# The first tile's load split over two DMA queues, and shorter idle matmuls ahead of it

## The chip, the core and the metric

The kernel runs on one NeuronCore of a Trainium2 chip. TensorE multiplies matrices from SBUF into PSUM, VectorE and ScalarE work on tiles, GpSimd does the rest, and SyncE issues most DMAs. ScalarE has a DMA queue of its own as well. The metric is the device time of one execution in microseconds (us); the median of three runs of the kernel before is 210.25 us (210.12 to 210.37).

## The reference

The input x has 2048 rows of 512 bf16 values. It is normalised row by row, and the result goes through linear attention of 32 heads and through a gated feed-forward layer of width 1792. Both are added to x.

```python
def _layernorm(x, axis=-1, eps=1e-5):
    m = jnp.mean(x, axis=axis, keepdims=True)
    v = jnp.var(x, axis=axis, keepdims=True)
    return (x - m) / jnp.sqrt(v + eps)

# linear attention: phi on q and k, k'v and the sum of k first, then q against them
phi = lambda t: jnp.where(t > 0, t + 1, jnp.exp(t)) + 1e-6
# feed-forward
(silu(x @ w_gate) * (x @ w_up)) @ w_down

xn = _layernorm(A_x)
return A_x + _A_ref(xn, A_wqkv, A_wo) + _B_ref(xn, B_w_gate, B_w_up, B_w_down)
```

## The kernel before

The 2048 rows are 16 tiles of 128 rows, one row to a partition. The program is written out by hand as one list of operations for each engine. A small planner (`_Prog`) keeps, for each named resource such as ("x", 0), who wrote it last and who has read it since; from that it derives every semaphore wait. Each engine works its own list strictly in order, so the place of a line in the source sets the order only among operations of the same engine. Each DMA has its own semaphore.

In the long run TensorE does, for each tile, the projections to k and q (line 438, with `kproj` and `qproj`), accumulates k'v (line 590), and later works the feed-forward layer (line 785) and the output (lines 979 and 990). The start is different, because nothing is in SBUF yet. The steps that matter are these.

- **Loads** (lines 199 to 262). SyncE loads tile 0 of x as its first DMA (line 250), then chunks 0 and 1 of the key weights in one load of 256 KB, chunk 2, tile 2, and so on. ScalarE's queue has two loads, tile 1 (line 239) and chunk 3 of the key weights (line 252). Ahead of them ScalarE has one Exp on a single column, which brings in its table (line 236). The load of tile 1 is declared as a reader of `ident`, so it waits for the memset of that tile on GpSimd (line 238), and GpSimd's next write of `ident`, the select that makes the identity matrix (line 242), waits until that load has landed.
- **Idle matmuls** (`fill`, line 267). TensorE begins with eight matmuls of constants, 512 columns wide, whose result nobody reads (line 610), and has one of 128 columns among the transposes (line 620).
- **Tile 0**: VectorE takes the statistics (`bns`, line 299, and `agg`, line 302) and subtracts the mean in two halves of the columns into `xc_sb` (`xc_half`, line 382). TensorE transposes each half against `ident` in two matmuls (`tp_first`, line 410), ScalarE copies it into `xcT` (`tc_first`, line 422).
- **Tile 1**: ScalarE takes the mean itself (`mean_act`, line 307), VectorE subtracts it after tile 0's halves, and the same transposes and copies follow.
- **First projections** (`proj_part`, line 465): one matmul for each chunk of the weights, for tile 0 in the order of chunks 0, 1, 3, 2, then the same for tile 1, then parts of the query projections. Tile 2 comes in after twelve of them, with four transposes.

The factor of the variance is put in later, by ScalarE's reading of the projections (`first_ek` and the like), so the transposes needn't wait for it. GpSimd computes it (`eps` and `rstd_of`) after `ident` and a memset of two values.

Of the kernel before, what the change touches and what calls it, by code (L numbers as in the profile page):

```python
# [10 lines left out]
P = 128  # L11
# [98 lines left out]
def bass_parallel_sum__linear_attn_block__swiglu_ffn__prompt_kernel(  # L110
# [10 lines left out]
    xin = A_x[0]  # L121
    oview = out[0]
    K = _Prog()
    pe, act, dve, pool, sp = nc.tensor, nc.scalar, nc.vector, nc.gpsimd, nc.sync
    bf, f32 = dt.bfloat16, dt.float32

    with contextlib.ExitStack() as es:
        E = es.enter_context

        def sb(name, shape, d=bf):  # L130
            return E(nc.sbuf_tensor(name, [P] + shape, d))

        x_sb = sb("x_sb", [NT, D])
# [14 lines left out]
        stats = sb("stats", [NT, 6], f32)  # L148
# [43 lines left out]
        def bk(i):  # L192
            return ("bank", i)
# [5 lines left out]
        def rows(v, t0, n):  # L199
            if t0 < NLONE:  # L200
                return v[t0 * P:(t0 + n) * P, :].rearrange("(t p) d -> p t d", p=P)
            return v[NLONE * P:, :].rearrange("(p t) d -> p t d", t=NT - NLONE)[:, t0 - NLONE:t0 - NLONE + n, :]

        def xload(eng, h, t0, n, after=()):
            K.dma(
                eng, lambda: h.dma_start(x_sb[:, t0:t0 + n, :], rows(xin, t0, n)),
                r=list(after), w=[("x", t0 + i) for i in range(n)],
            )

        def wqkv_load(eng, h, name, i, c0, n, after=()):  # L210
            K.dma(
                eng,
                lambda: h.dma_start(
                    wqkv_sb[:, c0:c0 + n, i * D:(i + 1) * D],
                    A_wqkv[c0 * P:(c0 + n) * P, i * D:(i + 1) * D].rearrange("(c p) f -> p c f", p=P),
                ),
                r=list(after), w=[(name, c) for c in range(c0, c0 + n)],
            )
# [6 lines left out]
        def whalf(name, dst, src, h):  # L225
# [6 lines left out]
                w=[(name, h)],  # L232
            )

        K.op("pool", lambda: pool.memset(warm[:, :], 0.0), w=[("warm",)])
        K.op("act", lambda: act.activation(warm[:, :], warm[:, :], ACT.Exp), r=[("warm",)], w=[("warm",)])

# [8 lines left out]
            r=[("ident",)], w=[("ident",)],  # L246
        )
        K.op("pool", lambda: pool.memset(nhalf[:, :], -0.5), w=[("nhalf",)])

        xload("sp", sp, 0, 1)  # L250
        wqkv_load("sp", sp, "wk", 1, 0, 2)
        wqkv_load("act", act, "wk", 1, 3, 1)
        wqkv_load("sp", sp, "wk", 1, 2, 1)
# [13 lines left out]
        def fill(n, cols, after=()):  # L267
            K.op(
                "pe",
                [  # L270
                    (lambda: pe.matmul(banks[3][:, 0:cols], cw, cx[:, 0:cols], start=True, stop=True))  # L271
                    for _ in range(n)
                ],
                r=list(after), w=[bk(3)],
            )
# [20 lines left out]


        def bns(t):
            K.op("dve", lambda: dve.bn_stats(stats[:, t, :], x_sb[:, t, :]), r=[("x", t)], w=[("st", t)])  # L299

        def agg(t):
            K.op("dve", lambda: dve.bn_aggr(mv[:, t, :], stats[:, t, :]), r=[("st", t)], w=[("mv", t)])
# [296 lines left out]
        def stat(t):  # L599
            bns(t)  # L600
            agg(t)
            eps(t, "pool")
            rstd_of(t)
# [3 lines left out]
            if t >= 3:  # L607
                transpose_dma(t)

        fill(8, 512)  # L610
        bns(0)
        agg(0)
        xc_half(0, 0)
# [10 lines left out]
        tp_first(1, 0, 6)  # L624
        tc_first(1, 0, 6)
        bns(1)
        rstd_of(0)
        xn_dve(0)
# [459 lines left out]
```

## Time and profile before

| | |
|---|---|
| median of 3 runs | 210.25 us (210.12 to 210.37) |
| the profiled execution | 210.51 us, of which 209.3 us are the span that the profile covers |
| TensorE busy | 206.6 us, 99% of the span |
| VectorE / ScalarE / GpSimd busy | 57% / 34% / 34% |
| DMA | 16.84 MB, mean 80 GB/s |

All times in a profile line are us from the start of the span, unless marked ns. In the timeline a line holds the start, the length, the engine, the source line and the operation with its tiles; neighbours of the same kind are merged (x3), the length is then from the first one's start to the last one's end, and the square bracket tells how long the engine had been idle before and what ended that. A question about a short window shows pieces that a longer one merges. PE is TensorE, PEld its loading of weights, DVE VectorE, ACT ScalarE, POOL GpSimd; SPq and ACTq are the issues of DMAs on SyncE's and ScalarE's queues. Matmuls are pipelined: the next one can start before the one before has its end in the profile.

### The profile page before, as it was taken

The page shows a single profiled execution, that of the slowest core. Times are in us where ns is not written, and L with a number is a line of the kernel's source. Part 1 is how long each engine was busy: PE and PEld are TensorE (multiplying, and loading weights), DVE is VectorE, ACT ScalarE, POOL GpSimd, SP SyncE. Part 2 cuts the span into 40 slices and gives each one's busy share as a digit, 9 for nine tenths or more (in the row PEclk, how much of TensorE's full clock was granted, in tenths as well). Part 3 has the DMA queues.
Part 4 walks back from the last instruction along what each step waited for, and adds up shares of the span by engine and source line. Part 5 has one row for each costly group of instructions (what it writes and reads, how often), then busy time and mean ns, then how long its engine had stood idle before and what let it go on. Part 6 is the DMA issues. An engine that isn't in the chain of part 4 may idle for free.

```text
span 209.3 us, 2824 instructions
## 1 busy us (share of the span) xinstructions
PE 206.6 (99%) x1015; PEld 94.6 (45%) x1015; DVE 120.2 (57%) x246; ACT 70.9 (34%) x125; POOL 72.0 (34%) x90
## 2 busy tenths in 40 slices
PE   8999999999999999999999999999999999999996
PEld 3444444444444444444444444444444444444444
DVE  3999988336365874637355746365556545374122
ACT  5777666966643331312112312213031213121000
POOL 3427977568032543223041422240424132221200
PEclk9999999999999999999999999999999999999999
DMA  6673644894797011010101110102011010110101
GB/s 200 209 195 75 127 100 100 256 364 158 202 357 50 11 39 25 28 25 25 50 2 50 28 29 22 50 0 53 6 45 25 27 28 25 49 30 25 50 28 50
DMA packets 30287, 16.84 MB, mean 80 GB/s; under 512 B 20928, under 2 KB 29632, under 8 KB 30272
## 3 DMA queue, kind: packets, MB, share of 16 engines
q1 hardware_dynamic: 29984, 16.39, 29.9%
q10 hardware_dynamic: 288, 0.26, 0.4%
q8 instruction: 8, 0.13, 0.2%
q14 instruction: 7, 0.06, 0.1%
HBM read 9.70 MB, written 2.10 MB: 56 GB/s over the span
## 4 chain that ended last, share of the span: by engine, by line
PE 99%; DVE 0%; issue 0%
PE psum L785 46%; PE psum L990 23%; PE psum L438 10%; PE psum L979 7%; PE psum L590 7%; PE psum L271 2%; PE psum L465 2%; PE psum L452 2%; PE psum L410 1%; PE psum L892 0%; PE psum L915 0%; DVE out_sb L1003 0%
## 5 line engine op out<-in xcount | busy, mean ns | idle before, releaser
L800 ACT ACTIVATE sg<-psum 128x512 bf16<-128x512 f32 x56 | 33.4, 598 | 106.0 <-PE psum L785 102.5
L785 PE MATMUL psum<-xnT,wg_sb 128*128 128x512 bf16 x224 | 57.5, 379 | 0.0
L785 PE MATMUL psum<-xnT,wu_sb 128*128 128x512 bf16 x224 | 57.5, 379 | 0.0
L934 POOL TENSOR_TENSOR prod<-pkq,zb 128x512 f32<-128x512 bf16 x16 | 18.6, 1163 | 55.9 <-DVE pkq L514 55.9
L785 PEld LDWEIGHTS psum<-xnT,wu_sb 128*128 128x128 bf16 x224 | 21.9, 98 | 26.4
L785 PEld LDWEIGHTS psum<-xnT,wg_sb 128*128 128x128 bf16 x224 | 21.8, 98 | 26.2 <-issue 0.2
L1003 DVE TENSOR_TENSOR out_sb<-psum,x_sb 128x512 bf16<-128x512 f32 (+2 forms) x17 | 11.2, 660 | 35.9 <-PE psum L990 35.9
L958 POOL TENSOR_TENSOR pqn<-pkq,rden 128x512 bf16<-128x512 bf16 x16 | 16.9, 1056 | 36.5 <-DVE rden L952 36.5
L806 DVE TENSOR_TENSOR pkq<-psum,sg 128x512 bf16<-128x512 f32 x28 | 19.2, 686 | 17.1 <-PE psum L785 14.7
L806 DVE TENSOR_TENSOR xn_sb<-psum,sg 128x512 bf16<-128x512 f32 x28 | 18.8, 673 | 14.1 <-PE psum L785 13.6
L990 PE MATMUL psum<-wd_sb,xn_sb 128*128 128x512 bf16 (+2 forms) x126 | 25.7, 355 | 0.0
L990 PE MATMUL psum<-wd_sb,pkq 128*128 128x512 bf16 x112 | 25.5, 379 | 0.0
L438 PE MATMUL psum<-wqkv_sb,xnT 128*128 128x512 bf16 x96 | 22.5, 379 | 0.0
L582 POOL TENSOR_TENSOR zacc<-zacc,pkq 128x512 f32<-128x512 f32 x15 | 17.3, 1155 | 5.0 <-DVE ek L505 4.6
L990 PEld LDWEIGHTS psum<-wd_sb,xn_sb 128*128 128x128 bf16 x126 | 11.8, 98 | 12.5
L990 PEld LDWEIGHTS psum<-wd_sb,pkq 128*128 128x128 bf16 x112 | 11.0, 98 | 13.2
L979 PE MATMUL psum<-m_sb,eq 128*128 128x512 bf16 (+2 forms) x68 | 16.6, 366 | 0.0
L590 PE MATMUL psum<-pkq,xn_sb 128*128 128x512 bf16 x64 | 15.9, 379 | 0.0
L438 PEld LDWEIGHTS psum<-wqkv_sb,xnT 128*128 128x128 bf16 x96 | 9.4, 98 | 11.3
L942 DVE TENSOR_REDUCE den<-prod 128x32 f32<-128x512 f32 x16 | 10.9, 683 | 5.9 <-POOL prod L934 5.9
L299 DVE BATCH_NORM_STATS2 stats<-x_sb 128x6 f32<-128x512 bf16 x16 | 10.9, 681 | 3.4 <-DMA x_sb<-in_A_x_dram 3.4
L514 DVE SCALAR_TENSOR_TENSOR pkq<-pkq,eq 128x512 bf16<-128x512 bf16 x16 | 11.1, 692 | 0.6
(68 smaller groups left out, 138.7 us busy)
## 6 DMA issues: line engine op xcount, KB each, us to landing
out_dram<-out_sb SPq DMA_DIRECT2D x15, 128.0 KB, 1.7
wg_sb<-in_B_w_gate_dram SPq DMA_DIRECT2D x2, 896.0 KB, 7.8
wu_sb<-in_B_w_up_dram SPq DMA_DIRECT2D x2, 896.0 KB, 6.1
wd_sb<-in_B_w_down_dram SPq DMA_DIRECT2D x1, 1792.0 KB, 11.1
x_sb<-in_A_x_dram SPq DMA_DIRECT2D x5, 256.0 KB, 3.1
x_sb<-in_A_x_dram SPq DMA_DIRECT2D x5, 128.0 KB, 3.4
wqkv_sb<-in_A_wqkv_dram SPq DMA_DIRECT2D x5, 128.0 KB, 3.8
wqkv_sb<-in_A_wqkv_dram SPq DMA_DIRECT2D x1, 512.0 KB, 7.9
```

Source lines behind the costliest of these rows:

```text
L438: (lambda c=c: pe.matmul(banks[b], xnT[:, c, t * P:(t + 1) * P], wqkv_sb[:, c, lo:lo + D], start=(c == 0), stop=(c == NDC - 1),))
L514: lambda: dve.scalar_tensor_tensor(out=dst, in0=src, scalar=0.0, in1=e, op0=ALU.max, op1=ALU.add,),
L582: lambda: pool.tensor_tensor(out=zacc[:, :], in0=zacc[:, :], in1=pk, op=ALU.add),
L590: (lambda c=c: pe.matmul(banks[4 + c], xn_sb[:, t, c * P:(c + 1) * P], pkq[:, t, 0, :], start=(t == 0), stop=(t == NT - 1),))
L785: (lambda c=c: pe.matmul(banks[b], w_sb[:, c, fc * P:(fc + 1) * P], xnT[:, c, C * 512:(C + 1) * 512], start=(c == 0), stop=(c == NDC - 1),))
L800: lambda: act.activation(sg[:, j % NSG, :], banks[gb], ACT.Silu),
L806: lambda: dve.tensor_tensor(out=hT(C, fc), in0=banks[ub], in1=sg[:, j % NSG, :], op=ALU.mult,),
L934: lambda: pool.tensor_tensor(out=p, in0=pkq[:, t, 1, :], in1=zb[:, :], op=ALU.mult),
L958: lambda: pool.tensor_tensor(out=pqn[:, t % NPN, :].rearrange("p (i g h e) -> p g i h e", i=NB, g=NG, e=DH), in0=pkq[:, t, 1, :].rearrange ...
L979: (lambda g=g: pe.matmul(dst, pqnT(t)[:, g, :], m_sb[:, g, lo:hi], start=(g == 0), stop=False,))
L990: (lambda fc=fc: pe.matmul(dst, hT(C, fc)[:, jj * P:(jj + 1) * P], wd_sb[:, fc, lo:hi], start=False, stop=(fc == NFC - 1),))
L1003: lambda: dve.tensor_tensor(out=o, in0=src, in1=x_sb[:, t, lo:hi], op=ALU.add),
```

## The change

Tile 0 of x is loaded by two DMAs of 64 rows (partitions 0 to 63 and 64 to 127), one from SyncE's queue and one from ScalarE's. On ScalarE's queue the half comes ahead of the Exp, and so ahead of the two loads that the queue had. On SyncE's queue it stands where the whole tile stood, as the first DMA. The half from ScalarE's queue is kept as a resource of its own, ("xb", 0); only `bns` reads it, and what follows on VectorE comes after that. The first run of idle matmuls is seven of 512 columns and one of 128 in place of eight of 512.

```diff
+        def xhalf(eng, h, t, lo, name):
+            K.dma(
+                eng, lambda: h.dma_start(x_sb[lo:lo + P // 2, t, :], rows(xin, t, 1)[lo:lo + P // 2, 0, :]),
+                w=[(name, t)],
+            )
+
+        xhalf("sp", sp, 0, 0, "x")
+        xhalf("act", act, 0, P // 2, "xb")
         K.op("pool", lambda: pool.memset(warm[:, :], 0.0), w=[("warm",)])
         K.op("act", lambda: act.activation(warm[:, :], warm[:, :], ACT.Exp), r=[("warm",)], w=[("warm",)])
...
-        xload("sp", sp, 0, 1)
         wqkv_load("sp", sp, "wk", 1, 0, 2)
         wqkv_load("act", act, "wk", 1, 3, 1)
...
         def bns(t):
-            K.op("dve", lambda: dve.bn_stats(stats[:, t, :], x_sb[:, t, :]), r=[("x", t)], w=[("st", t)])
+            K.op("dve", lambda: dve.bn_stats(stats[:, t, :], x_sb[:, t, :]), r=[("x", t), ("xb", t)], w=[("st", t)])
...
-        fill(8, 512)
+        fill(7, 512)
+        fill(1, P)
         bns(0)
```

## The prediction

> **What bounds the kernel now.** I began with the chain of waits, because it tells whose delay reaches the end.
>
> ```profile
> PE 99%; DVE 0%; issue 0%
> ...
> 0.84 3.57 PE psum L271 x8
> 4.41 0.36 PE psum L410 x2
> ...
> 4.87 0.64 PE psum L410 x6
> 5.51 2.75 PE psum L465 x12
> ...
> 9.35 1.73 PE psum L452 x8
> ...
> 206.65 0.80 PE psum L990 x14
> ...
> 207.47 0.29 DVE out_sb L1003
> ```
>
> Columns are start, length, work, in us. TensorE is on the chain from 0.84 to 207.45, each piece beginning where the one before ended. The eight idle matmuls of L271 run to 4.41, 3.57 in all, while eight of the same width at 9.35 take 1.73, or 0.216 each; the six 128-column transposes before 5.51 take 0.64/6 = 0.107 each. The twelve at 5.51 would take 12 x 0.216 = 2.59 at the later rate and take 2.75. So TensorE works at half rate until about 5.4 to 5.5 and at full rate afterwards. From there on it runs with hardly a gap, so the end is fixed by when that run begins: the change is worth what it moves that moment, not what it saves before.
>
> The timeline of the first 6 us, asked in short windows, shows what the run waits for:
>
> ```profile
> 0.80 1.28 ACT L236 ACT_TABLE_LOAD   x1 [0.80 <-PEq L1073]
> 0.80 0.39 SPq L206 DMA_DIRECT2D x_sb<-in_A_x_dram  x1
> 1.07 0.38 ACTq L206 DMA_DIRECT2D x_sb<-in_A_x_dram  x1
> 1.25 0.41 SPq L213 DMA_DIRECT2D wqkv_sb<-in_A_wqkv_dram  x1
> 1.48 0.45 ACTq L213 DMA_DIRECT2D wqkv_sb<-in_A_wqkv_dram  x1
> 1.72 0.46 SPq L213 DMA_DIRECT2D wqkv_sb<-in_A_wqkv_dram  x1
> ...
> 2.92 1.48 PE L271 MATMUL psum<-const-bfloat16-1.0 128*128 128x512 bf16 x3
> 3.08 0.69 DVE L299 BATCH_NORM_STATS2 stats<-x_sb 128x6 f32<-128x512 bf16 x1 [3.08 <-DMA x_sb<-in_A_x_dram]
> 3.37 0.63 ACT L307 ACTIVATE scr<-x_sb 128x512 bf16<-128x512 bf16 x1 [1.08 <-DMA x_sb<-in_A_x_dram]
> 3.57 0.29 POOL L242 TENSOR_SCALAR_AFFINE_SELECT ident<-ident 128x128 bf16<-128x128 bf16 x1 [2.54 <-DMA x_sb<-in_A_x_dram]
> 3.91 0.19 ACT L307 ACTIVATION_READ_ACCUMULATOR scr<-x_sb 128x1 f32 x1
> 4.03 0.48 DVE L382 TENSOR_SCALAR xc_sb<-x_sb,mv 128x256 bf16<-128x256 bf16 x2
> 4.37 0.13 PEld L410 LDWEIGHTS psum<-ident,xc_sb 128*128 128x128 bf16 x2 [0.87 <-DVE xc_sb L382]
> 4.42 0.48 DVE L382 TENSOR_SCALAR xc_sb<-x_sb,mact 128x256 bf16<-128x256 bf16 x2
> ...
> 4.80 0.70 ACT L422 ACTIVATE xcT<-psum 128x256 bf16<-128x256 bf16 x2 [0.71 <-PE psum L410]
> 5.31 0.66 PE L465 MATMUL psum<-wqkv_sb,xcT 128*128 128x512 bf16 x2
> 5.91 0.34 PEld L465 LDWEIGHTS psum<-wqkv_sb,xcT 128*128 128x128 bf16 x3 [0.45 <-ACT xcT L422]
> 5.94 1.02 PE L465 MATMUL psum<-wqkv_sb,xcT 128*128 128x512 bf16 x4
> ```
>
> Three readings. **First**, the fillers don't hold the first transpose. The last of them, some 0.63 long with its tail, ends at 4.40, so it starts at 3.77; starts are (3.77-0.84)/7 = 0.42 apart, and the array is free at 4.19. The transpose starts at 4.37, released by VectorE's xc_sb: 0.18 late. **Second**, GpSimd's ident waits until tile 1's load has landed (the load was declared a reader of ident) and ends at 3.57+0.29 = 3.86. **Third**, the two projections at 5.31 end at 5.97; the second is 0.38 long, starts at 5.59 and frees the array at 5.81, but the third starts at 5.94. The row names ScalarE's xcT, yet the two copies it could need ended at 4.80+0.70 = 5.50. What is left is weight chunk 3, loaded from ScalarE's queue at 1.48:
>
> ```profile
> x_sb<-in_A_x_dram SPq DMA_DIRECT2D x1, 128.0 KB, 2.3
> x_sb<-in_A_x_dram ACTq DMA_DIRECT2D x1, 128.0 KB, 2.3
> wqkv_sb<-in_A_wqkv_dram SPq DMA_DIRECT2D x1, 256.0 KB, 2.9
> wqkv_sb<-in_A_wqkv_dram ACTq DMA_DIRECT2D x1, 128.0 KB, 4.3
> wqkv_sb<-in_A_wqkv_dram SPq DMA_DIRECT2D x1, 128.0 KB, 4.3
> ...
> 1.50:2.00 0.50, 0.50 (x2) 0.15 (x1) 0.00 (x0) 0.50 (x1) 0.00 (x0) 1.00 0.14 43
> 2.00:2.50 0.50, 0.50 (x3) 0.15 (x1) 0.00 (x0) 0.28 (x2) 0.00 (x0) 1.00 0.87 299
> 2.50:6.00 3.50, 3.50 (x17) 1.62 (x15) 2.76 (x9) 1.92 (x6) 1.30 (x4) 1.00 1.00 313
> ```
>
> The upper rows are DMA issues with KB and us to landing, the lower ones stretches with the DMA engines' busy share and GB/s at the end. Chunk 3 took 4.3 where tile 1 took 2.3: it lands at 1.48+4.3 = 5.78, and TensorE goes on 0.16 later. Chunk 2, SyncE's load at 1.72 that the fourth projection needs at 5.94+0.216 = 6.16, lands at 6.02, just as close. The DMA engines are full from 2.50 to 6.00. So the gapless run is held by two weight loads in a full queue, and tile 0 stands only 5.94-5.81 = 0.13 in front of it.
>
> **The change part by part.**
> *Fillers.* Seven of 512 and one of 128 free the array at 0.84 + 7 x 0.42 + 0.107 = 3.89, 0.30 sooner. This alone gains nothing, since xc_sb comes at 4.37. If xc_sb stays there, the array idles 0.48 in place of 0.18, at no cost of its own while 5.94 holds.
> *Tile 0.* Two loads of 64 KB replace one of 128 KB; both can be issued at 0.80. No row shows a 64 KB load. Stores give a slope:
>
> ```profile
> out_dram<-out_sb SPq DMA_DIRECT2D x1, 96.0 KB, 1.6
> out_dram<-out_sb SPq DMA_DIRECT2D x1, 32.0 KB, 1.4
> ```
>
> That is 0.2 per 64 KB; the step from 2.3 to 2.9 between 128 and 256 KB gives 0.3. The other half needs the same engines, but they were 0.14 busy up to 2.00, and ahead of tile 1's bytes now. Bounds: 0 (the halves share what the whole had) and -0.5 (both slopes together). I take -0.3, the rows of loads rather than stores. VectorE now waits for two semaphores there; it has nothing else to do before, so the second check is costed at nothing, and what is queued behind it is the whole chain counted here. Statistics then start at 2.78, and xc_sb allows a transpose at 4.07.
>
> [...]
>
> *ScalarE's queue.* Its half goes ahead of everything there: one issue of 0.38 from 0.80. The table load ahead of Exp may move by as much, to 0.80+0.38+1.28 = 2.46 and Exp behind it; nothing needs ScalarE until tile 1's mean at 3.37. Tile 1's load moves from 1.07 to about 1.22, chunk 3's from 1.48 to 1.63: +0.15 each. SyncE issues the same number of loads at the same places, and an issue's length hardly follows its size (0.39 for 128 KB, 0.41 for 256), so its queue stays.
> *Tile 1* lands +0.15: ident is done at 4.01 in place of 3.86, still below 4.07, so the first transpose gains 0.28 to 0.30. The mean of tile 1 ends at 3.91+0.19+0.15 = 4.25, so its xc_sb starts at about 4.27 in place of 4.42; its transposes, and the first projection queued behind them, gain 0.15. Bounds for tile 1: -0.05 (fewer bytes of tile 0 beside it) and +0.6 (the 256 KB issued at 1.25 slip in ahead, 2.9 against 2.3).
> *The third projection.* By the matmuls it could start at 5.81-0.15 = 5.66; by chunk 3 at 5.94 plus the shift of that landing. Upper bound +0.2 (64 KB more ahead of it in its own queue at the 313 GB/s of the row, 0.21; its issue, +0.15, lies within). Lower bound: the bytes ahead in both queues are the same in sum, and the second queue starts up to 0.27 sooner (0.80 against 1.07) on engines idle before 2.00, so -0.27; then 5.67. Chunk 2 has 64 KB less ahead on SyncE's queue: -0.21 to 0. I take -0.05 for both, near the middle of chunk 3's bounds. Tile 2 is covered:
>
> ```profile
> 7.18 0.48 DVE L382 TENSOR_SCALAR xc_sb<-x_sb,mv 128x256 bf16<-128x256 bf16 x2
> 8.10 0.28 PE L410 MATMUL psum<-ident,xc_sb 128*128 128x128 bf16 x2
> ```
>
> Tile 2 is ready at 7.66 and wanted at 8.10: 0.44 of cover, which is also the most that can be gained before it binds.
> *Sum:* fillers 0, tile 0's lead hidden behind the weights, run start 5.94 - 0.05 = 5.89. The profiled execution took 210.51 (span 209.3 and 1.2 around it), which is 0.26 over the median of 210.25; the step applies to both, so I forecast **210.2**, with 209.95 to 210.45 for this case alone.
>
> **The rivals.**
> *A, faster: the weights come early too.* Tile 0 near its bound of -0.5, tile 1 unchanged (mean done at 4.10), so xc_sb of tile 1 starts at 4.12, 0.30 sooner, and the third projection could start at 5.51; if chunks 3 and 2 both land early enough, 0.43 is gained, just under tile 2's cover: 209.8. For it speaks that 4.3 is long for 128 KB; against it, the full engines, and that two loads from two queues must come early together.
> *B, slower: the full rate comes later.* TensorE doubled its rate about 4.6 us after its first matmul, after 4.19-0.84 = 3.35 of unbroken fillers and one gap of 0.18. With fillers to 3.89 and tile 0 not at 4.07, or with chunk 3 late behind earlier projections, the gaps grow to 0.5 or more. It decides if such a gap starts the count anew: from 4.1 another 4.6 leads to 8.7, and the work between 5.94 and 8.7 at half rate costs 2.76/2 = 1.4: 211.6. For it: half rate is plain in the rows. Against: the 0.18 did no such thing.
>
> [...]
>
> *C: tile 1 late.* At its +0.6, ident ends at 4.46 and tile 1's mean at 4.70; its transposes end near 5.48 and the third projection comes at 5.9 to 6.0: 210.25 to 210.3, or 210.45 with chunk 3 late.
> *D: the load isn't quicker.* Tile 0 at 3.08 again; the run starts at 5.94 to 6.09: 210.25 to 210.4.
>
> **How the numbers follow.** The forecast has 0.40, A 0.22, B 0.18, C 0.08, D 0.12. About 0.2% (0.42) is what a measurement of this kernel can tell from no change. A is faster by that: 0.22. Forecast, C and D lie within it, but 0.07 of C and D goes where a larger gap also delays the rate a little: within 0.53, slower 0.18+0.07 = 0.25. The range 209.75 to 210.85 takes in A with the bounds and half-sized delays, and leaves out B's full price.
>
> **What would show it.** The fillers' end near 4.1, statistics of tile 0 near 2.78, the first transpose near 4.07, tile 1's mean near 3.52, the first projection near 5.16 and the third still waiting near 5.9 would bear me out. The third projection starting below 5.6 is A; a 512-column projection pitch of 0.42 beyond 6 is B; a select of ident after 4.1 is C; statistics still at 3.08 are D. I am wrong if the gapless run moves by more than 0.4 for a reason that isn't among these.

## The result and the profile after

The changed kernel is slower by 0.6 to 1.1%, which is small but clear of the noise. Its median over ten runs is 211.62 us (210.99 to 213.46), beside 210.25 us for the kernel before (210.07 to 210.68, ten runs); the ratio is 1.0087, with a 95% interval of 1.006 to 1.0113. The ten times don't lie around one value: six are between 210.99 and 211.63, four between 212.49 and 213.46. The profiled execution took 213.05 us (span 211.8), one of the upper four; it is 2.5 longer in its span than that of before (209.3).

The timeline of the changed kernel's start, in short windows, holds the rows that answer to those of the prediction.

```profile
0.80 0.58 SPq L237 DMA_DIRECT2D x_sb<-in_A_x_dram  x1
0.81 0.57 ACTq L237 DMA_DIRECT2D x_sb<-in_A_x_dram  x1
...
1.44 0.57 SPq L213 DMA_DIRECT2D wqkv_sb<-in_A_wqkv_dram  x1
1.49 0.79 ACTq L206 DMA_DIRECT2D x_sb<-in_A_x_dram  x1
...
3.31 0.69 DVE L306 BATCH_NORM_STATS2 stats<-x_sb 128x6 f32<-128x512 bf16 x1 [3.31 <-DMA x_sb<-in_A_x_dram]
...
5.00 0.63 ACT L314 ACTIVATE scr<-x_sb 128x512 bf16<-128x512 bf16 x1 [2.08 <-DMA x_sb<-in_A_x_dram]
5.20 0.29 POOL L250 TENSOR_SCALAR_AFFINE_SELECT ident<-ident 128x128 bf16<-128x128 bf16 x1 [4.16 <-DMA x_sb<-in_A_x_dram]
...
5.64 0.37 PE L417 MATMUL psum<-ident,xc_sb 128*128 128x128 bf16 x2 [1.54 <-POOL nhalf L256]
...
5.75 0.48 DVE L389 TENSOR_SCALAR xc_sb<-x_sb,mact 128x256 bf16<-128x256 bf16 x2 [1.01 <-ACT scr L314]
...
6.55 0.63 PE L472 MATMUL psum<-wqkv_sb,xcT 128*128 128x512 bf16 x1
```

Each half takes 0.57 to 0.58 to issue, where the whole tile took 0.39. So tile 1's load, behind ScalarE's half, is issued at 1.49 in place of 1.07: after SyncE's 256 KB weight load (1.44) and no longer ahead of it (1.07 against 1.25). The statistics of tile 0 start at 3.31 in place of 3.08. ScalarE's mean of tile 1, which waits for that load, starts at 5.00 in place of 3.37; the select of `ident`, which waits for it too, ends at 5.49 in place of 3.86. The first transpose comes at 5.64 in place of 4.37, and what it waited for is GpSimd (the row names the small memset behind the select of `ident`), no longer VectorE; the first projection comes at 6.55 in place of 5.31, 1.24 later.

The DMA issues of the same kernel (KB of each, us to landing) show where tile 1's time went.

```profile
x_sb<-in_A_x_dram SPq DMA_DIRECT2D x1, 64.0 KB, 2.2
x_sb<-in_A_x_dram ACTq DMA_DIRECT2D x1, 64.0 KB, 2.4
wqkv_sb<-in_A_wqkv_dram SPq DMA_DIRECT2D x1, 256.0 KB, 3.3
x_sb<-in_A_x_dram ACTq DMA_DIRECT2D x1, 128.0 KB, 3.5
```

Half of tile 0 takes about as long as the whole took (2.3). Tile 1 takes 3.5 from issue to landing, 2.3 before; 1.49 + 3.5 is 5.0, and the 256 KB in front of it land at 1.44 + 3.3 = 4.7. Of tile 1's delay of 1.6, 0.4 is thus its later issue and 1.2 its longer way.

The chain of waits says the same; it no longer starts on TensorE.

```profile
1.49 3.49 DMA x_sb<-in_A_x_dram
...
6.76 4.04 PE psum L472 x12
```

The twelve projections after the start take 4.04 of the chain, 2.75 before. The timeline says why. Its rows here are the loads of weights into the array (one ahead of each projection) and the four transposes of tile 2.

```profile
9.11 0.15 PEld L472 LDWEIGHTS psum<-wqkv_sb,xcT 128*128 128x128 bf16 x1 [0.28 <-issue]
9.54 0.76 PEld L472 LDWEIGHTS psum<-wqkv_sb,xcT 128*128 128x128 bf16 x4 [0.28 <-issue]
10.63 0.39 PE L417 MATMUL psum<-ident,xc_sb 128*128 128x128 bf16 x4
```

Up to 9.54 they are 0.43 apart (9.11 to 9.54), and from there four take 0.76. So TensorE works at half rate until about 9.5 to 9.7, not until 5.4. Tile 2's transposes start at 10.63 in place of 8.10: 2.53 later, all of the difference in the spans. Of this the first projection's 1.24 is the start that comes late; the other 1.29 is lost between there and tile 2, at half rate.

### The profile page after: what moved, and what is told of

Its sections match the earlier page's. It is cut to its first block, busy times and chain, and to the rows that moved or that the text cites. A ratio compares the mean times of both kernels' runs of the same rounds, so it can differ in the third digit from the quotient of the medians.

```text
span 211.8 us, 2826 instructions
## 1 busy us (share of the span) xinstructions
PE 207.6 (98%) x1015; PEld 94.9 (45%) x1015; DVE 120.4 (57%) x246; ACT 70.9 (33%) x125; POOL 72.0 (34%) x90
## 4 chain that ended last, share of the span: by engine, by line
PE 96%; DMA 2%; ACTq 0%; issue 0%; POOL 0%; DVE 0%; ACT 0%; POOLq 0%
PE psum L793 46%; PE psum L998 23%; PE psum L445 10%; PE psum L987 7%; PE psum L597 7%; PE psum L472 2%; DMA x_sb<-in_A_x_dram 2%; PE psum L459 2%; PE psum L417 1%; PE psum L900 0%; ACTq L237 0%; PE psum L923 0%; POOL ident L250 0%; DVE out_sb L1011 0%; PE psum L278 0%
```

## The experiments

**The theories.** T: the loss has two parts. Tile 1's load is issued behind a half of tile 0 in its own queue and behind the 256 KB of weights in the other, and lands 1.6 late, which delays both `ident` and tile 1's mean, and so the run of projections; and the array then stands idle between fillers and transposes (4.1 to 5.64), after which the full rate comes late in part of the executions, which would be the two groups of times. S is its first link, that the half loads themselves push tile 1 back; at first I took the two queues' simultaneous issues for the cause (the collision). F, the rival: it is the shortened fillers that bring the rate late. Another rival is that `ident`, tied to tile 1's load, is the whole delay.

### One part of the change at a time

**The split alone**, with the eight fillers of before.

```diff
-        fill(7, 512)
-        fill(1, P)
+        fill(8, 512)
```

> The split load with the eight idle matmuls of 512 columns of the kernel before. Theory T (tile 1's load is late behind the half on ScalarE's queue and behind the 256 KB of weights, and TensorE then stands idle until 5.6 us, which also puts off its full rate): tile 1's mean begins near 5.0, ident's select near 5.2, the first projection near 6.5; time 211.2 to 212.5 with a wide spread. Rival F (the shorter idle matmuls open the gap that costs the time): 210.1 to 210.5. Rival L (the half loads land late by themselves, statistics at 3.3 in place of 3.1): 210.4 to 210.6.

213.14 us (210.91 to 214.51, ten runs), ratio 1.0112 (1.0083 to 1.0141). The load alone costs all that the change costs, and the eighth long filler doesn't mend it.

**The fillers alone**, in the kernel before.

```diff
-        fill(8, 512)
+        fill(7, 512)
+        fill(1, P)
```

> The kernel before with seven idle matmuls of 512 and one of 128 columns; the load of tile 0 is whole. Theory T: nothing lands later, the array idles 0.48 in place of 0.18 us before the first transpose at 4.37; time 210.1 to 210.5. Rival F (the gap alone delays the full rate): 211 to 212, with projections 0.42 apart after 6 us. Rival L: 210.25.

210.2 us (210.03 to 210.98), ratio 0.9999 (0.9986 to 1.0013). Its timeline:

```profile
3.78 0.31 PE L271 MATMUL psum<-const-bfloat16-1.0 128*128 128x128 bf16 x1
...
4.28 0.29 PE L410 MATMUL psum<-ident,xc_sb 128*128 128x128 bf16 x2 [0.18 <-DVE xc_sb L382]
...
5.04 2.76 PE L465 MATMUL psum<-wqkv_sb,xcT 128*128 128x512 bf16 x12
7.64 0.39 PE L410 MATMUL psum<-ident,xc_sb 128*128 128x128 bf16 x4
```

The fillers end at 4.09, the gap of 0.18 costs no rate (twelve projections in 2.76 are 0.216 apart), and F falls: shorter fillers alone cost nothing. The full rate is even there by the first transposes, whose two take 0.29 from 4.28, so it came over 1 us sooner than in the profile of before.

### The two parts of the loss taken apart

**Lateness without idleness**: the changed kernel with eleven fillers, so that the array works until shortly before the transposes.

```diff
-        fill(7, 512)
+        fill(11, 512)
```

> The split load with eleven idle matmuls of 512 columns, which reach to about 5.5 us. Theory T: the full rate is there from about 5.4 us again, the first projection still at 6.5 because tile 1 is late. The run then begins 6.55 - (5.94 - 2 x 0.216) = 1.04 us later than before: 211.3, and the spread of the changed kernel (210.99 to 213.46) shrinks to some 0.5. If lateness of tile 1 were the whole cause: the same spread and median as the changed kernel (211.6). If the rate were the whole cause: 210.25.

211.53 us (211.41 to 211.59, four runs), ratio 1.0049 (1.0033 to 1.0065). None of the four runs is in the upper group; they lie within 0.18. Its timeline:

```profile
4.63 0.76 PE L278 MATMUL psum<-const-bfloat16-1.0 128*128 128x512 bf16 x2
...
6.58 2.75 PE L472 MATMUL psum<-wqkv_sb,xcT 128*128 128x512 bf16 x12
9.17 0.39 PE L417 MATMUL psum<-ident,xc_sb 128*128 128x128 bf16 x4
```

The fillers run to 5.39, the projections start as late as in the changed kernel but at full rate at once, and tile 2's transposes come at 9.17 in place of 8.10: 1.07 late. That is the price of the lateness alone; the time says 1.2 over the before of the same runs (210.31).

**Idleness without lateness**: the kernel before with four fillers, so that every load and every tile is on time.

```diff
-        fill(8, 512)
+        fill(4, 512)
```

> The kernel before with four idle matmuls of 512 columns in place of eight: the array idles from about 2.55 to 4.37, 1.8 us, as long as in the changed kernel (3.9 to 5.6), and nothing else is touched. Theory T: loads and first projection stay (5.0 to 5.3), but the full rate comes later, with projections 0.42 apart beyond 6 us in part of the executions: 210.8 to 212.5, spread over 1 us. If the idle array costs nothing: 210.1 to 210.5, spread as the kernel before.

211.6 us (211.34 to 211.84, four runs), ratio 1.0054 (1.0034 to 1.0074). Its timeline:

```profile
4.30 0.39 PE L410 MATMUL psum<-ident,xc_sb 128*128 128x128 bf16 x2 [1.60 <-DVE xc_sb L382]
...
5.24 0.63 PE L465 MATMUL psum<-wqkv_sb,xcT 128*128 128x512 bf16 x1
...
9.43 0.39 PE L410 MATMUL psum<-ident,xc_sb 128*128 128x128 bf16 x4
```

The first projection is even 0.07 early, but from there to tile 2's transposes it takes 4.19, where before it took 8.10 - 5.31 = 2.79. The rate alone costs 1.33 at that point. The array had been idle for 1.60; in the changed kernel it was 1.54. All four runs are slow by about as much, so the wide spread that was expected didn't show.

**The changed kernel once more**, for a second profile.

> The changed kernel once more, for a second profile: its executions fall into two groups, near 211.0 to 211.6 and near 212.5 to 213.5. Theory T: in an execution of the lower group the projections after 6.5 us are 0.216 apart, in one of the upper group 0.42 apart up to about 9.5, with the first projection at 6.5 to 6.9 in both.

This execution took 211.43 us, one of the lower group. Its timeline:

```profile
5.00 0.63 ACT L314 ACTIVATE scr<-x_sb 128x512 bf16<-128x512 bf16 x1 [2.09 <-DMA x_sb<-in_A_x_dram]
...
6.42 2.75 PE L472 MATMUL psum<-wqkv_sb,xcT 128*128 128x512 bf16 x12
9.01 0.39 PE L417 MATMUL psum<-ident,xc_sb 128*128 128x128 bf16 x4
```

Tile 1 is just as late (5.00), yet the twelve projections go through at full rate, and tile 2's transposes come at 9.01 against 10.63 in the first profile: 1.62, as much as the spans differ (210.2 and 211.8). These two executions, one of each group, are one program with the same late load; they differ in when the rate doubles. The lateness alone is 9.01 - 8.10 = 0.91 here.

### What makes tile 1 late

**`ident` untied** in the changed kernel.

```diff
-        xload("act", act, 1, 1, [("ident",)])
+        xload("act", act, 1, 1)
```

> The changed kernel with tile 1's load and ident not waiting for one another. Tile 1's load keeps its place on ScalarE's queue. If tile 1's mean is what holds the first projection (theory T): ident is ready before 2, tile 0's transposes begin near 4.6, but tile 1 still lands near 5.0 and the first projection stays at 6.3 to 6.6: 211.0 to 212.5. If ident's wait is what costs: first projection below 5.6 and 210.2 to 210.6.

212.78 us (211.0 to 213.43, four runs), ratio 1.0101 (1.0053 to 1.0149): nothing is won. The first transpose comes at 4.57, but the timeline goes on:

```profile
5.34 0.63 ACT L314 ACTIVATE scr<-x_sb 128x512 bf16<-128x512 bf16 x1 [2.44 <-DMA x_sb<-in_A_x_dram]
...
6.84 0.63 PE L472 MATMUL psum<-wqkv_sb,xcT 128*128 128x512 bf16 x1
```

Tile 1's own mean still waits until 5.34, and the first projection stands behind tile 1's transposes. `ident` is not the whole delay; tile 1's landing holds the run without it.

**Both halves on SyncE's queue**, so that no two issues of halves run at once and ScalarE's queue is as before.

```diff
-        xhalf("act", act, 0, P // 2, "xb")
+        xhalf("sp", sp, 0, P // 2, "xb")
```

> The changed kernel with both halves of tile 0 issued from SyncE, one behind the other; ScalarE's queue is that of the kernel before (tile 1 at 1.07, chunk 3 at 1.48). Theory T, now with its first link (two loads issued at the same moment from two queues slow each other's issue, 0.58 in place of 0.39): each half is issued in about 0.4, tile 1 lands near 3.4 to 3.5, tile 0's statistics begin near 3.5 (the second half is issued 0.45 later), the first projection comes by 5.5: 210.2 to 210.9. If half loads were slow by themselves wherever they are issued: as the changed kernel, 211 to 213, tile 1 near 5.0.

212.88 us (211.37 to 213.12, four runs), ratio 1.0104 (1.0065 to 1.0143); not expected. Its timeline:

```profile
0.80 0.58 SPq L237 DMA_DIRECT2D x_sb<-in_A_x_dram  x1
...
1.44 0.57 SPq L237 DMA_DIRECT2D x_sb<-in_A_x_dram  x1
...
4.32 0.69 DVE L306 BATCH_NORM_STATS2 stats<-x_sb 128x6 f32<-128x512 bf16 x1 [4.32 <-DMA x_sb<-in_A_x_dram]
```

A half with no other half beside it takes 0.58 to issue too, so that collision is not what makes it long. Tile 1 is on time here, its mean at 3.47; it is tile 0 that comes late (4.32), with the first projection at 6.55 again. Its second half, issued at 1.44 and ahead of all weights, took 2.8 to land, so a load can be long on its way without the weights ahead of it.

**Two whole loads at once**: in the kernel before, tile 1's load no longer waits for the memset of `ident`.

```diff
-        xload("act", act, 1, 1, [("ident",)])
+        xload("act", act, 1, 1)
```

> The kernel before with tile 1's load free of ident, so that the whole loads of tile 0 (SyncE) and tile 1 (ScalarE) are issued at the same moment, 0.80. Theory T: both issues take 0.55 to 0.6 in place of 0.39, tile 0's statistics begin near 3.3 in place of 3.0 to 3.1, tile 1 lands by 3.6, the first projection moves by 0.1 to 0.3: 210.2 to 210.8. If the slow issue belongs to half loads alone: issues of 0.39, statistics at 3.0 to 3.1, 210.1 to 210.4.

210.5 us (210.1 to 210.98), ratio 1.0003 (0.9989 to 1.0017). The timeline:

```profile
0.81 0.40 SPq L206 DMA_DIRECT2D x_sb<-in_A_x_dram  x1
...
0.94 0.39 ACTq L206 DMA_DIRECT2D x_sb<-in_A_x_dram  x1
...
5.76 0.15 PEld L465 LDWEIGHTS psum<-wqkv_sb,xcT 128*128 128x128 bf16 x1 [0.28 <-ACT xcT L422]
...
6.19 0.82 PEld L465 LDWEIGHTS psum<-wqkv_sb,xcT 128*128 128x128 bf16 x4 [0.28 <-issue]
```

Two whole loads, overlapping on the two queues, take 0.39 and 0.40 to issue. The collision falls; what is left is the half itself, by its 64 rows or by its 64 KB. The run shows one thing more: with nothing late and hardly a gap, the loads of weights ahead of its projections were still 0.43 apart up to 6.19, so its rate doubled later than in the profile of before (5.4 to 5.5).

**64 rows in mid-stream**: in the kernel before, tile 4's load, which nothing early waits for, is made of two halves.

```diff
-        xload("sp", sp, 4, 1)
+        xhalf("sp", sp, 4, 0, "x")
+        xhalf("sp", sp, 4, P // 2, "xb")
```

> The kernel before with tile 4's load (SyncE, near 5.1 us, 0.43 to issue) split into two of 64 rows, tile 0 whole. Theory S: each of the two takes 0.55 to 0.6 to issue; the later loads slip by about 0.7; the time stays within 0.4 of before. If only the first loads of a queue are slow: 0.43 each.

One run, 210.84 us. The timeline:

```profile
5.07 0.56 SPq L237 DMA_DIRECT2D x_sb<-in_A_x_dram  x1
5.68 0.59 SPq L237 DMA_DIRECT2D x_sb<-in_A_x_dram  x1
6.31 0.58 SPq L206 DMA_DIRECT2D x_sb<-in_A_x_dram  x1
6.93 0.43 SPq L206 DMA_DIRECT2D x_sb<-in_A_x_dram  x1
```

The halves take 0.56 and 0.59 and the whole load right behind them 0.58; the next takes 0.43 again, as tile 4's load did there before. The half of 64 rows is slow in mid-stream too.

**Halves by columns**: all 128 rows, 256 columns each, in the same places of the two queues.

```diff
-                eng, lambda: h.dma_start(x_sb[lo:lo + P // 2, t, :], rows(xin, t, 1)[lo:lo + P // 2, 0, :]),
+                eng, lambda: h.dma_start(x_sb[:, t, lo:lo + D // 2], rows(xin, t, 1)[:, 0, lo:lo + D // 2]),
...
-        xhalf("act", act, 0, P // 2, "xb")
+        xhalf("act", act, 0, D // 2, "xb")
```

> The changed kernel with tile 0 split by columns in place of rows: two loads of 128 rows x 256 columns, 64 KB each, from the same queues at the same places. Theory S (the slow issue belongs to the 64-row form: every 64-row load so far took 0.56 to 0.58 to issue, alone or beside another, every 128-row load at the start 0.38 to 0.40): issues near 0.4, tile 0's statistics by 3.1, but tile 1 still behind the 256 KB on ScalarE's queue if that is issued first; time 210.3 to 211.5. Theory C (issuing at the same moment from two queues, or 64 KB loads as such, are slow): issues 0.55 or more, statistics at 3.3, 211 to 213.5.

212.8 us (211.02 to 213.15), ratio 1.0092 (1.0063 to 1.0121). The halves' issues, both at 0.80, are down to 0.39 and 0.40: neither the 64 KB nor the common moment makes an issue long, and the 64 rows are left. But tile 1 is issued at 1.30, still just behind the 256 KB at 1.25:

```profile
1.30 0.40 ACTq L206 DMA_DIRECT2D x_sb<-in_A_x_dram  x1
...
4.78 0.63 ACT L314 ACTIVATE scr<-x_sb 128x512 bf16<-128x512 bf16 x1 [2.06 <-DMA x_sb<-in_A_x_dram]
```

The mean of tile 1 starts at 4.78. A load that is issued 0.23 later than before (1.30 against 1.07) lands 1.4 later. The long issue is thus only one way to get there; a short one does it too. Nor is tile 0 sooner: the halves land after 2.2 and 2.4, as those of 64 rows did, and its statistics start at 3.26, where 3.1 was expected. So the long issue is not what keeps tile 0 from coming early.

**The order alone**: the kernel before, with whole loads and all its fillers; ScalarE's two loads change places.

```diff
-        xload("act", act, 1, 1, [("ident",)])
+        wqkv_load("act", act, "wk", 1, 3, 1, [("ident",)])
...
-        wqkv_load("act", act, "wk", 1, 3, 1)
+        xload("act", act, 1, 1)
```

> The kernel before with whole loads and eight fillers; only the order of ScalarE's queue is changed: chunk 3 of the weights first (with the wait for the ident), tile 1 behind it. If what delays tile 1 is only that its load is issued behind SyncE's 256 KB weight load, tile 1 lands at 4.4 or later instead of 3.35, its mean starts there, the first projection starts at 6.0 to 6.5, and the time is 211 to 213 us without any half load in the kernel. If the half loads themselves are needed for the loss, tile 1 lands before 3.9 and the time is 210.1 to 210.5.

213.16 us, the median of five runs (211.42, 211.71, 213.16, 213.19 and 213.46; a sixth took 565.09 us and isn't counted), ratio 1.009 (1.0057 to 1.0123). The timeline:

```profile
1.07 0.38 ACTq L213 DMA_DIRECT2D wqkv_sb<-in_A_wqkv_dram  x1
...
1.48 0.45 ACTq L206 DMA_DIRECT2D x_sb<-in_A_x_dram  x1
...
4.85 0.63 ACT L307 ACTIVATE scr<-x_sb 128x512 bf16<-128x512 bf16 x1 [2.56 <-DMA x_sb<-in_A_x_dram]
...
5.96 0.61 PE L410 MATMUL psum<-ident,xc_sb 128*128 128x128 bf16 x4 [0.76 <-DVE xc_sb L382]
...
10.76 0.39 PE L410 MATMUL psum<-ident,xc_sb 128*128 128x128 bf16 x4
```

Without any half load, tile 1, issued at 1.48 behind SyncE's 256 KB (and behind chunk 3 in its own queue), is late by 1.5 (4.85), the times fall into the same two groups, and the loss is about the same. In this profiled execution the array stood idle for only 0.76 ahead of tile 1's transposes, and the rate came late all the same (tile 2 at 10.76).

The column halves and this run change two things at once for tile 1: it has the 256 KB ahead of it on SyncE's queue, and it is the second load of its own queue, no longer the first. No run parts the two for tile 1, but the two runs below that move it to SyncE put chunk 3 of the weights, also 128 KB, in that second place, ahead of the 256 KB. With column halves (issues of 0.41) chunk 3, issued at 1.30, took 2.7 to land there, where tile 1 behind the 256 KB took 3.5. With row halves, issued at 1.48 in 0.79, it took 3.3, where tile 1 in the changed kernel, issued in 0.79 as well, took 3.5. First on its queue, tile 1 took 2.3. So with short issues most of the longer way goes with the weights ahead; behind a half of 64 rows most of it is there without them. How the 1.2 of the changed kernel divides stays open.

### Tile 1 ahead of the weights

**On SyncE's queue, right behind its half** of 64 rows, in the changed kernel.

```diff
-        xload("act", act, 1, 1, [("ident",)])
+        xload("sp", sp, 1, 1)
```

> The changed kernel with tile 1's load issued from SyncE's queue right behind SyncE's half of tile 0 and ahead of the 256 KB of weights, without waiting for ident; ScalarE's queue keeps its half and weight chunk 3. Theory T: tile 1 lands by 3.8, the transposes run from about 4.3, the first projection below 5.5: 210.0 to 210.6. Rival L (the halves themselves): 210.4 to 210.6, statistics of tile 0 at 3.3. Rival F (the short fillers): 211 or more.

211.18 us (210.82 to 212.68, ten runs, two of them at 212.7), ratio 1.0046 (1.0022 to 1.007): better than the split alone, but not level. Two rows of its timeline:

```profile
3.80 0.63 ACT L314 ACTIVATE scr<-x_sb 128x512 bf16<-128x512 bf16 x1 [0.89 <-DMA x_sb<-in_A_x_dram]
...
8.24 0.39 PE L417 MATMUL psum<-ident,xc_sb 128*128 128x128 bf16 x4
```

The mean of tile 1 starts at 3.80, and tile 2's transposes are only 0.14 late. The rest is lost behind them, and the chain of waits tells where:

```profile
1.43 0.56 SPq L206
...
5.90 3.87 DMA x_sb<-in_A_x_dram
```

It runs through SyncE's issues: one load more and two slow ones at its head (0.58 for the half, 0.56 for tile 1) push back all that follows there, and the last of them on the chain, a load of later tiles issued at 5.90, is one for which VectorE then waits. That load was issued at 5.07 before, and at 5.56 with the column halves of the next run: of the 0.83, about 0.49 is the added load and 0.34 the slow issues. Mending the landing of tile 1 moved the cost onto the rest of that queue.

**The same with halves by columns.**

```diff
-        xhalf("act", act, 0, P // 2, "xb")
+        xhalf("act", act, 0, D // 2, "xb")
-        xload("act", act, 1, 1, [("ident",)])
+        xload("sp", sp, 1, 1)
```

> As the column halves, with tile 1's load on SyncE's queue right behind its half and free of ident. By theory S tile 0's statistics begin by 3.1 and tile 1 lands by 3.6, so this would be at least level with the kernel before: 210.0 to 210.5. By theory C it is as the row halves with tile 1 on SyncE: 210.8 to 211.3.

210.62 us (210.52 to 211.08), ratio 1.0013 (1.0002 to 1.0024). With both causes gone, the long issues and the late tile 1 (its mean starts at 3.77), tile 0 is still split over two queues and nearly nothing is lost. Nothing is won either:

```profile
5.36 3.01 PE L472 MATMUL psum<-wqkv_sb,xcT 128*128 128x512 bf16 x12
...
6.25 1.63 PEld L472 LDWEIGHTS psum<-wqkv_sb,xcT 128*128 128x128 bf16 x9 [0.50 <-DMA wqkv_sb<-in_A_wqkv_dram]
```

Tile 0's statistics start at 3.18 and not by 3.1, the first projection comes at 5.36, as before (5.31), and the fourth waits for its weights (the load into the array after 0.50 of idleness).

**Whole loads, tile 1 second on SyncE's queue**, and two weight chunks on ScalarE's: the one version that might have beaten both kernels.

```diff
-        xload("act", act, 1, 1, [("ident",)])
+        xload("sp", sp, 1, 1)
...
-        wqkv_load("act", act, "wk", 1, 3, 1)
-        wqkv_load("sp", sp, "wk", 1, 2, 1)
+        wqkv_load("act", act, "wk", 1, 3, 1, [("ident",)])
+        wqkv_load("act", act, "wk", 1, 2, 1)
```

> The kernel before with whole loads and eight fillers; tile 1 is SyncE's second load, right behind tile 0, ahead of the 256 KB weight load, and ScalarE's queue carries two chunks of weights. If the landing of tile 1 sets the first projection, tile 1 lands at 3.4 to 3.8 and the first projection starts at 5.2 to 5.5 as before: 209.9 to 210.4, level or slightly better. If the weights, now issued later, come late instead, the first projections wait for them: 210.5 to 211.5.

210.65 us, the median of eleven runs (210.42 to 213.42), beside 210.68 for the before of the same runs, ratio 1.0021 (0.9996 to 1.0045): not told from level, and no better. Its profile is of a twelfth run, of 273.92 us, which isn't counted, and isn't read. No version here beat the kernel before.

## Why the prediction was wrong

The forecast was 210.2, 0.05 less than before, within 209.75 to 210.85; the median is 211.62, 1.37 more than before. The step that failed stands under ScalarE's queue, and its consequences behind it.

*What bounds the kernel.* Half right. What delays the first tiles delays the end by as much: the 2.53 at tile 2's transposes are the 2.5 between the spans. But the beginning of the run moved by only 1.24; the prediction took the full rate from 5.4 to 5.5 on as given, and the rest is that it wasn't there. That moment isn't fixed even without a late tile: by 4.3 with the shorter fillers alone, after 6.19 with the two whole loads at once.

*Fillers.* Right: alone they change nothing, and in the profile their last row ends at 4.09, near the sign of 4.1.

*Tile 0, -0.3.* Wrong in sign: the statistics start 0.23 later, 3.31. Both bounds lay on one side, since I let a half cost at most what the whole cost: an estimate, as no row of before had a 64 KB load. The halves take 2.2 and 2.4 to land where the whole took 2.3, by rows and by columns alike.

*ScalarE's queue: the step that failed.* "An issue's length hardly follows its size" was read from 128 and 256 KB, both in loads of 128 rows; the 64-row form takes 0.57. With 0.38 the prediction had tile 1 issued at 1.22, three hundredths ahead of the 256 KB at 1.25; it was issued at 1.49, behind them, 0.42 later than before in place of 0.15. And the margin alone was too thin for a point value: the column halves, with issues of 0.40, had tile 1 at 1.30, behind the weights as well, since 0.10 passed between the two issues.

*Tile 1, bounds -0.05 to +0.6.* Its mean came 1.63 late (5.00 against 3.37). I had named a mechanism, the 256 KB slipping in ahead, but priced it by the weights' own 2.9 against 2.3. The nearer row stood in the prediction: chunk 3, issued at 1.48 behind the 256 KB and second on ScalarE's queue, took 4.3. Tile 1 now has about that load's place in the order, and took 3.5. By the row of chunk 3 the bound would have been 1.48 + 4.3 - (1.07 + 2.3) = +2.4; +0.6 left the measured value out. That the weights ahead are all of it is not shown, as the second place on the queue came with them.

*What follows tile 1.* The links were right: both `ident` and the mean hang on it, `ident` ends after 4.1, which was the sign for rival C, and with `ident` untied the first projection is late all the same. Only their input was mis-sized.

*The third projection.* Its wait for weights is gone. It follows the second at half rate, and the profile shows no wait for a load there; whatever the halves did to chunks 3 and 2 is covered.

*The rivals.* C had the place and the wrong size. B had the price nearly right (1.4; measured 1.33 with four fillers, and 1.62 between the two profiles of the changed kernel). What failed is that I took them for two cases that exclude each other. The late tile of C opens the idle stretch that B needs; B's gap came from tile 1, not from tile 0's lead. Added up, 0.9 to 1.1 for lateness and 1.3 to 1.6 for the rate in some of the executions give 210.25 + 1.1 = 211.35 at most for the one group and 212.45 to 212.95 for the other, near the measured 210.99 to 211.63 and 212.49 to 213.46. B's point from which it decides, a gap of 0.5, isn't a rule: gaps of 0.18 to 0.53 cost no rate in the profiles and 0.76 did in one, but about 1.5 cost it in one execution of the changed kernel (1.54) and not in another (1.58).

## What to carry to other kernels

When an edit puts an issue in front of others on a DMA queue, list the order in which all queues' early loads are issued, before and after; where two issues are within some tenths of a us, price the flip by a row of a load that already stands in that place, behind the big one and second on its queue. A wait that idles TensorE near its start may cost twice, once as lateness (0.9 to 1.1 here) and once as the rate (1.3 to 1.6 here); idle matmuls that lasted through the wait (eleven here) left only the first cost in four runs (1.2 in the time). Don't carry the cost of an operation over from another shape: here a load of half the rows was dearer to issue (0.57 to 0.58) than a whole one (0.39).

## What the runs showed of the hardware

- A load of 64 rows took 0.56 to 0.59 us to issue, on either queue, alone or beside another, at the start or in mid-stream; one of 128 rows of x took 0.38 to 0.47, for 64 KB (half the columns) as for 128, where no 64-row load stood right ahead of it. Loads right behind 64-row ones took longer as well (0.57 for the 256 KB that took 0.41 before, 0.79 for tile 1 that took 0.38). Why isn't shown.
- In the crowded start (the DMA engines are 1.00 busy from 2.50 to 6.00 in the profile of before, 0.97 in that of the changed kernel), 0.23 us of delay in issuing 128 KB became 1.4 in landing, where the load came behind another queue's 256 KB and second on its own. Second on that queue but ahead of the 256 KB, 128 KB took 2.7 to land (3.3 where it also came behind a half of 64 rows), against 3.5 behind them and 2.3 first on the queue.
- The moment at which TensorE doubles its rate (loads of weights ahead of the projections 0.43 apart, then about 0.22) varies between executions of one program. After some 1.5 us of idleness the changed kernel had the full rate at 5.64, with the first transposes, in one profile (its first two take 0.27) and only after 9.5 in another (there they take 0.37). Between kernels without a long gap it varied too, from 4.3 or less (the fillers alone) to after 6.19 (two whole loads at once); these two profiled executions took 210.05 and 210.83 us. The granted clock doesn't tell the two executions of the changed kernel apart. The row of the slower one, for the microsecond from 8.00, reads

```profile
8.00:9.00 1.00, 1.00 (x4) 0.30 (x2) 0.96 (x4) 0.50 (x1) 0.79 (x2) 1.00 0.96 333
```

and in the faster one

```profile
8.00:9.00 1.00, 1.00 (x6) 0.42 (x5) 0.96 (x4) 0.75 (x2) 0.79 (x2) 1.00 1.03 359
```

with 1.00 in both (the third figure from the end), though four matmuls ran in the one and six in the other. What decides the moment, and so the group, in a given execution stays open.
